# Idle TensorE products in the gaps of a fused SSD and squared-ReLU FFN kernel, with one load and one product group moved

## The chip, the cores and the metric

The kernel runs on one core of one Trainium2 chip. Its time is the device time of one execution in microseconds (us); the median over several executions is what is compared. Each core has TensorE (PE, matrix products, results in PSUM), VectorE (DVE), ScalarE (ACT), GpSimd (POOL) and SyncE (SP). Here SP and POOL issue nearly all DMA transfers. A product is preceded by a weight load, which the profile lists as PEld.

## The reference

A state-space layer (chunked scan with decay) feeds an FFN with a squared ReLU. Cut to what matters:

```python
# x (4,8,768,32)  a (4,8,768)  B, C (4,8,768,16); in chunks of 32 positions
M       = einsum('bhin,bhjn->bhij', Cc, Bc) * exp(cum_i - cum_j) * causal
y_intra = einsum('bhij,bhjd->bhid', M, xc)
y_inter = einsum('bhin,bhnd->bhid', Cc, state) * exp(cum_i)
y       = y_intra + y_inter
state   = exp(sum(log a)) * state + sum_j Bc_j * xc_j * exp(cum_last - cum_j)
# y as (3072, 256), w_in (256, 2048), w_out (2048, 256)
h   = maximum(y @ w_in, 0)
out = (h * h) @ w_out
```

The output is 3072 x 256 in float32.

## The kernel before

The 3072 tokens are cut into 12 pairs, each 256 tokens of one batch (`PAIRS`; two halves of 128 tokens, `u`, with their own state). For each pair k there is a state-space part and an FFN block.

State-space part of pair k, in this order:

- `ph_load`: three DMAs into `C_nat`, `B_nat` and `x_nat` (128, 128 and 256 KB), from a ring of four buffers each (`nat`). SP issues them, only B of pair 0 is issued by ACT.
- `ph_prep` (`prep_c`, `prep_b`, `prep_x`): C times the running decay into `cz`, B cast into `Bb`, x over the running decay into `xs`. For pairs from 2 on POOL does all three; for pairs 0 and 1 ACT does B and DVE does C.
- `ph_tr`: six transposes on PE, copied by DVE into `bct`. `ph_mt`: 16 products of C and B (`mt`). `ph_mask`: four causal masks on DVE into `mts`. For pair 0 two of them read a copy made by ACT (`mtc`).
- `ph_u`: 16 products of B and x (`U`). `ph_s`: DVE makes the states `S` from U and the total decay `Ptot`.
- `ph_y`: first the products of `bct` with the state (line 264), then 32 products of `mts` with `xs` (line 276), all summed in PSUM as `Y`, then evicted into `T`. For pair 0 only the second half has a state.

FFN block of pair b, eight steps f: `mm1` (four 256-wide products `hps` with two of the 16 slices of `w_in`, then a ReLU on ACT into `hb`), `square` (DVE, one step later, into `h`), `mm2` (four products `ops` with two slices of `w_out`, four steps later, `LAG`). At the last step ACT evicts `ops` and SP stores it.

The order is written out by hand (`manual_schedule`), with one running count of steps s = 8b + f. The dictionary `todo` says at which step what part of a later pair is issued; `at(s, ...)` adds to it. Every engine works through its instructions in order and waits for the semaphores that each of them needs; a tile's buffer is taken from a ring (the pool), and the writer waits for the readers of whatever held the buffer before.

Ahead of step 0 there is a stretch by hand: the loads of pairs 0 to 3 on SP; on POOL the constants `cb`, the first quarter of `w_in`, `prep_x(0)`, then the other weights by quarters (`load_wi` in slices 4 to 8, 8 to 12, 12 to 16, `load_wo` in slices 0 to 4, 4 to 8, 8 to 16) with `prep_x(1)` between them. The weights are float32 in memory and bfloat16 in the tiles. `w_in` slices 4 to 8 are first read at step 2, slices 8 to 12 at step 4, 12 to 16 at step 6; `w_out` slices 0 to 4 at step 4, 4 to 8 at step 6, 8 to 16 at step 8.

`warm(n, cols)` issues n products of a tile of zeros, `dum`, into a PSUM tile `dps` that nothing reads: 16 of 256 columns at the start, 3 behind the transposes of the decay (`ptr`), 5 of 128 columns behind `ph_tr(0)` and 14 behind `ph_u(0)`.

Of the kernel before, what the change touches and what calls it, by code (L numbers as in the profile page):

```python
# [10 lines left out]
FP32 = mybir.dt.float32  # L11
# [19 lines left out]
def kernel(  # L31
# [14 lines left out]
    nc = tc.nc  # L46
    NH, S, D, N = 8, 768, 32, 16
    NPAIR = 12
    LAG = 4
    LEAD = 10  # L50

    const = ctx.enter_context(tc.tile_pool(name="const", bufs=1))
    wpool = ctx.enter_context(tc.tile_pool(name="w", bufs=1))
    nat = ctx.enter_context(tc.tile_pool(name="nat", bufs=4))
    prep = ctx.enter_context(tc.tile_pool(name="prep", bufs=3))
    big = ctx.enter_context(tc.tile_pool(name="big", bufs=2))
    tpool = ctx.enter_context(tc.tile_pool(name="tpool", bufs=4))
# [31 lines left out]
    a_nat = const.tile([96, 256], FP32, name="a_nat")  # L89
    a_cl = const.tile([96, 256], FP32, name="a_cl")  # L90
    dum = const.tile([128, 256], BF16, name="dum")
    zer = const.tile([96, 128], FP32, name="zer")
    cp_r = const.tile([96, 256], FP32, name="cp_r")
    pick_p = const.tile([96, 2, 12], FP32, name="pick_p")
# [13 lines left out]
    loaded = {}  # L108
# [17 lines left out]
    def load_wo(f0, f1):  # L126
        nc.gpsimd.dma_start(  # L127
            out=w_out_b[:, f0:f1, :],
            in_=moe_w_out[f0 * 128:f1 * 128, :].rearrange("(f p) d -> p f d", p=128))


    live = {}
# [95 lines left out]
    def ph_s(k, us=(0, 1)):  # L228
# [3 lines left out]
        for u in us:  # L232
# [10 lines left out]
            S_u.append(S_n)  # L243
            state[b] = S_n

    T = {}

    def ph_y(k):
        b, j = PAIRS[k]
        v = live[k]  # L250
        if k < 1:
            Y = [ps_s.tile([128, 2, 128], FP32, tag="A", name=f"Y{k}_{u}", padded_shape=[128, 8, 128])
                 for u in range(2)]
        else:
            t = ps_s.tile([128, 2, 4, 128], FP32, tag="A", name=f"Y{k}")
            Y = [t[:, u, 0:2, :] for u in range(2)]
        first = {(u, q): True for u in range(2) for q in range(4)}
        for u in range(2):
            S_b = v["S"][u]
            if S_b is None:  # L260
                continue
            for g in range(2):
                for q in range(4):
                    nc.tensor.matmul(  # L264
                        Y[u][32 * q:32 * q + 32, g, :],
                        S_b[32 * q:32 * q + 32, g * 32:(g + 1) * 32],
                        _fap(v["bct"][32 * q:32 * q + 32], 128 + g * 128 + u * 64, [[384, 2], [1, 64]]),
                        start=first[(u, q)], stop=False, skip_group_check=True,
                        tile_position=(32 * q, 32 * q))
                    first[(u, q)] = False  # L270
        for g in range(2):
            for r in range(2):
                for u in range(2):
                    for q in range(4):
                        h = 4 * g + q
                        nc.tensor.matmul(  # L276
                            Y[u][32 * q:32 * q + 32, g, :],
                            v["xs"][64 * u:64 * u + 64, r, h * 32:h * 32 + 32],
                            v["mts"][64 * u:64 * u + 64, q, r, g, :],
                            start=first[(u, q)], stop=(g == 1 and r == 1), skip_group_check=True,  # L280
                            tile_position=(64 * u, 32 * q))
                        first[(u, q)] = False
        if 2 <= k < NPAIR - 1:
            ph_u(k + 1)

        T[k] = tpool.tile([128, 2, 2, 2, 64], BF16, tag="T", name=f"T{k}")
        if k < 1:
            for u in range(2):
                o, i = _fap(T[k], u * 64, [[128, 4], [1, 64]]), _fap(Y[u], 0, [[64, 4], [1, 64]])
                if u:  # L290
                    nc.vector.tensor_copy(out=o, in_=i)
                else:
                    nc.scalar.copy(out=o, in_=i)
        else:
            nc.scalar.copy(out=_fap(T[k], 0, [[64, 2], [128, 4], [1, 64]]),  # L295
                           in_=_fap(Y[0], 0, [[512, 2], [64, 4], [1, 64]]))
# [57 lines left out]
    with tc.manual_schedule():  # L354
        nc.sync.dma_start(out=a_nat, in_=_dap(a, 0, [[256, 96], [1, 256]]))
        nc.scalar.dma_start(out=cf, in_=cf_d.ap())
        ph_load(0, "C")
        ph_load(0, "B", nc.scalar)
        ph_load(0, "x")
        nc.gpsimd.dma_start(out=cb, in_=cb_d.ap())  # L360
        load_wi(0, 4)
        for k in (1, 2, 3):
            ph_load(k)

        nc.vector.memset(dum, 0.0)  # L365
        nc.vector.memset(zer, 0.0)
        for i in range(3):
            nc.vector.memset(cz[i], 0.0)
        dps = ps_o.tile([128, 256], FP32, tag="ops", name="dps", padded_shape=[128, 512])

        def warm(n, cols=256):
            for _ in range(n):
                nc.tensor.matmul(dps[:, 0:cols], dum[:, 0:128], dum[:, 0:cols],  # L373
                                 start=True, stop=True, skip_group_check=True)

        warm(16)
        nc.vector.tensor_scalar(out=a_cl, in0=a_nat, scalar1=1e-6, scalar2=1.0, op0=ALU.max, op1=ALU.min)
        for u in range(2):
            nc.vector.tensor_tensor_scan(out=cp_r[:, u * 128:(u + 1) * 128], data0=a_cl[:, u * 128:(u + 1) * 128],
                                         data1=zer, initial=1.0, op0=ALU.mult, op1=ALU.add)  # L380
        nc.vector.tensor_tensor(out=pick_p, in0=_fap(pick, 0, [[0, 2], [1, 12]]),
                                in1=_fap(cp_r, 127, [[128, 2], [0, 12]]), op=ALU.mult)
        ptr = ps_h.tile([128, 2, 96], FP32, tag="hps", name="ptr", padded_shape=[128, 2, 256])
        for r in range(2):
            nc.tensor.transpose(ptr[:, r, :], _fap(cp_r, r, [[2, 128]]), eye_f)
        warm(3)
        pps = ps_h.tile([128, 2, 12], FP32, tag="hps", name="pps", padded_shape=[128, 2, 256])
        nc.tensor.matmul(pps, spread, pick_p, start=True, stop=True)
        nc.scalar.copy(out=P_sb, in_=ptr)
        prep_b(0, nc.scalar)  # L390
        nc.scalar.copy(out=Ptot, in_=pps)
        prep_c(0, nc.vector)
        nc.vector.reciprocal(out=_fap(Pinv, 0, [[96, 2], [3, 32]]), in_=_fap(P_sb, 0, [[96, 2], [3, 32]]))
        prep_x(0, nc.gpsimd)
        load_wi(4, 8)
        load_wo(0, 4)
        load_wi(8, 12)
        load_wo(4, 8)
        ph_tr(0)
        warm(5, 128)  # L400
        ph_mt(0)
        mtc = big.tile([128, 2, 2, 2, 128], BF16, tag="mtc", name="mtc", bufs=1)
        for i in (1, 0):
            nc.scalar.copy(out=mtc[:, i], in_=live[0]["mt"][1][:, i])
        ph_mask(0, 0)
        ph_u(0)
        warm(14, 128)
        ph_mask(0, 1)
        ph_s(0, (0,))
        ph_mask(0, 3, mtc[:, 1])  # L410
        ph_mask(0, 2, mtc[:, 0])
        prep_b(1, nc.scalar)
        prep_c(1, nc.vector)
        prep_x(1, nc.gpsimd)
        load_wi(12, 16)
        load_wo(8, 16)
        ph_y(0)
        ph_s(0, (1,))

        steps = [(b, f) for b in range(NPAIR) for f in range(8)]  # L420
        todo = {}

        def at(s, fn, *args):
            todo.setdefault(max(s, 0), []).append((fn, args))

        def recip_rest():
            nc.vector.reciprocal(out=_fap(Pinv, 1, [[96, 2], [3, 32], [1, 2]]),
                                 in_=_fap(P_sb, 1, [[96, 2], [3, 32], [1, 2]]))

        at(5, recip_rest)  # L430
        for k in range(1, NPAIR):
            s0 = {1: 0, 2: 7}.get(k, 8 * k - LEAD)
            if k >= 4:
                at(s0 - 15, ph_load, k)
            if k >= 2:
                at(s0 - {2: 6, 3: 5}.get(k, 7), ph_prep, k)
            at(s0, ph_tr, k)
            if k <= 2:
                at(s0 + 1, ph_u, k)
            at(s0 + 1 if k <= 2 else s0 - 1, ph_s, k)  # L440
            at(s0 + 2, ph_mt, k)
            for q in range(4):
                at(s0 + 2 + (q + 1) // 2, ph_mask, k, q)
            at(s0 + (5 if k == 1 else 6), ph_y, k)
        for s in range(len(steps) + LAG):
            if s < len(steps):
                mm1(*steps[s])
            for fn, args in todo.pop(s, []):
                fn(*args)
            if 1 <= s < len(steps) + 1:  # L450
                square(*steps[s - 1])
            if LAG <= s < len(steps):
                mm2(*steps[s - LAG])
        mm2_last(NPAIR - 1, [f for _, f in steps[len(steps) - LAG:]])
# [30 lines left out]
```

## Time and profile before

| what | value |
|---|---|
| median of 6 runs | 128.56 us (127.26 to 129.69) |
| profiled execution: its time | 128.67 us |
| profiled execution: its span | 126.9 us, 4221 instructions |
| mean granted TensorE clock | 0.946 |
| PE busy | 116.1 us (91%) |
| DVE, ACT, POOL busy | 88.4, 72.4, 32.1 us |
| chain that ended last | PE 70%, DMA 12%, DVE 11%, POOL 2% |

The span runs from the first instruction to the last; the rest of the execution's time lies around it. Busy time of PE is modelled and its instructions overlap, so a full PE in a slice says that it has no gap there. The granted clock is the share of full speed that the throttle gave TensorE. The chain is followed back from the last instruction, at each step to what released it. In the timeline's rows the first number is the start, the second the length, and brackets hold the idle time of the engine ahead of the row and what ended it.

### The profile page before, as it was taken

To read this page: it belongs to the slowest core of one execution; us is meant where nothing else is said; L and a number is where in the kernel's file an instruction comes from. 1 tells how busy PE (TensorE), PEld (TensorE's weight loads), DVE (VectorE), ACT (ScalarE), POOL (GpSimd) and SP (SyncE) were. 2 spreads that over 40 slices of the span, in tenths; PEclk is the share of its full clock that TensorE was granted. 3 is DMA by queue.
4 is the path that set the end of the run, shared out by engine and by line. 5 is a ranking of instruction groups with operands and counts; after the bars stand their busy time and mean duration, and the time that the engine had idled before them with its cause. 6 is when DMAs were issued, how large, how long until landed. Compare 5 with 4: busy or idle time off the path is not lost.

```text
span 126.9 us, 4221 instructions
## 1 busy us (share of the span) xinstructions
PE 116.1 (91%) x1778; PEld 92.7 (73%) x1778; DVE 88.4 (70%) x207; ACT 72.4 (57%) x129; POOL 32.1 (25%) x54
## 2 busy tenths in 40 slices
PE   6747849999999999999999999999999999999970
PEld 4525415778778978787888789788888887788840
DVE  3666588179989679599798795794865957934520
ACT  4232332456558557657576485585585675867720
POOL 5049942164052060430430430511500000000000
PEclk9997555699999999999999999999999999999999
DMA  4999999970830743905606507317220020020211
GB/s 81 205 196 148 185 206 214 212 141 3 182 71 10 161 85 92 161 5 132 121 3 152 101 0 167 86 52 138 64 83 8 0 90 3 5 83 0 88 41 41
DMA packets 42788, 12.10 MB, mean 95 GB/s; under 512 B 37808, under 2 KB 41344, under 8 KB 42768
## 3 DMA queue, kind: packets, MB, share of 16 engines
q1 hardware_dynamic: 38240, 9.28, 36.4%
q0 software_dynamic: 3232, 2.20, 12.0%
q10 hardware_dynamic: 1296, 0.35, 1.3%
q8 instruction: 14, 0.23, 0.7%
q14 instruction: 6, 0.05, 0.1%
HBM read 10.77 MB, written 3.15 MB: 110 GB/s over the span
## 4 chain that ended last, share of the span: by engine, by line
PE 70%; DMA 12%; DVE 11%; POOL 2%; ACT 1%; SPq 1%; issue 1%; DVEq 0%; POOLq 0%
PE ops L326 29%; PE hps L306 28%; DMA w_in_b<-in_moe_w_in_dram 7%; DVE mts L201 6%; DMA x_nat<-in_x_dram 5%; DVE h L316 5%; PE Y L276 3%; PE mt L190 3%; PE Y L264 2%; PE tr L178 2%; PE ops L339 1%; PE U L219 1%; PE tr L176 1%; POOL xs L157 1%; POOL w_out_b L127 1%
## 5 line engine op out<-in xcount | busy, mean ns | idle before, releaser
L310 ACT ACTIVATE hb<-hps 128x512 bf16<-128x512 f32 x96 | 57.5, 599 | 40.1 <-PE hps L306 39.1
L306 PE MATMUL hps<-T,w_in_b 128*128 128x256 bf16 x384 | 60.7, 283 | 2.8 <-DMA w_in_b<-in_moe_w_in_dram 1.7
L326 PE MATMUL ops<-w_out_b,h 128*128 128x256 bf16 x368 | 56.4, 277 | 0.0
L316 DVE TENSOR_TENSOR h<-hb 128x512 bf16<-128x512 bf16 x96 | 43.1, 472 | 6.5 <-ACT hb L310 6.5
L306 PEld LDWEIGHTS <-w_in_b 128*128 128x128 bf16 x384 | 38.3, 101 | 9.2 <-DMA w_in_b<-in_moe_w_in_dram 2.8
L326 PEld LDWEIGHTS <-h 128*128 128x128 bf16 x368 | 34.2, 99 | 6.6 <-issue 2.2
L201 DVE TENSOR_TENSOR mts<-mt,cb 128x512 bf16<-128x512 f32 x46 | 30.4, 682 | 8.3 <-PE mt L190 8.3
L137 POOL TENSOR_TENSOR cz<-C_nat,P_sb 128x256 bf16<-128x256 f32 x10 | 7.0, 696 | 42.9 <-DMA C_nat<-in_C_dram 36.7
L157 POOL TENSOR_TENSOR xs<-x_nat,Pinv 128x512 bf16<-128x512 f32 x12 | 13.0, 1083 | 10.3 <-DMA x_nat<-in_x_dram 10.1
L180 DVE COPY bct<-tr 128x768 bf16<-128x768 bf16 x12 | 6.7, 558 | 12.0 <-PE tr L178 11.7
L151 POOL CAST Bb<-B_nat 128x128 bf16<-128x128 f32 x20 | 6.4, 347 | 5.2 <-DMA B_nat<-in_B_dram 5.2
L295 ACT CAST T<-Y 128x512 bf16<-128x512 f32 x11 | 6.4, 586 | 1.7 <-PE Y L276 1.4
L351 ACT COPY osb<-ops 128x512 f32<-128x512 f32 x11 | 6.4, 579 | 0.0
L276 PE MATMUL Y<-mts,xs 64*32 64x128 bf16 x384 | 6.0, 226 | 0.4 <-DVE mts L201 0.3
L373 PE MATMUL dps<-dum 128*128 128x256 bf16 (+1 forms) x38 | 5.3, 301 | 1.1 <-DVE dum L365 1.1
L190 PE MATMUL mt<-bct 32*64 32x256 bf16 x192 | 5.3, 291 | 0.4 <-DVE bct L180 0.4
L178 PE MATMUL tr<-cb,cz 128*128 128x128 bf16 x48 | 5.6, 227 | 0.0
L176 PE MATMUL tr<-cb,Bb 128*128 128x128 bf16 x24 | 4.9, 228 | 0.4 <-ACT Bb L149 0.4
L373 PEld LDWEIGHTS <-dum 128*128 128x128 bf16 x38 | 3.7, 119 | 2.0 <-DVE dum L365 1.1
L276 PEld LDWEIGHTS <-xs 64*32 64x32 bf16 x384 | 3.4, 93 | 2.2 <-issue 1.0
L219 PE MATMUL U<-xs,Bb 64*32 64x64 bf16 x160 | 3.5, 199 | 1.5 <-POOL xs L157 1.5
L242 DVE TENSOR_SCALAR S<-z,Ptot 128x64 bf16<-128x64 f32 x16 | 4.3, 270 | 0.6
(40 smaller groups left out, 45.0 us busy)
## 6 DMA issues: line engine op xcount, KB each, us to landing
x_nat<-in_x_dram SPq DMA_DIRECT2D x12, 256.0 KB, 4.4
out_dram<-osb SPq DMA_DIRECT2D x11, 256.0 KB, 2.3
C_nat<-in_C_dram SPq DMA_DIRECT2D x12, 128.0 KB, 3.8
B_nat<-in_B_dram SPq DMA_DIRECT2D x11, 128.0 KB, 4.3
w_in_b<-in_moe_w_in_dram POOLq DMA_DIRECT2D x4, 256.0 KB, 7.2
w_out_b<-in_moe_w_out_dram POOLq DMA_DIRECT2D x2, 256.0 KB, 8.6
w_out_b<-in_moe_w_out_dram POOLq DMA_DIRECT2D x1, 512.0 KB, 11.9
B_nat<-in_B_dram ACTq DMA_DIRECT2D x1, 128.0 KB, 4.5
```

The source lines that it names most:

```text
L137: eng.tensor_tensor(out=_fap(czk, 0, [[240, 2], [32, 8], [1, 16]]), in0=_fap(loaded[k]["C"], 0, [[16, 2], [32, 8], [1, 16]]), in1=_fap(P_s ...
L157: eng.tensor_tensor(out=_fap(xs, 0, [[256, 2], [32, 8], [1, 32]]), in0=_fap(loaded[k]["x"], 0, [[32, 2], [64, 8], [1, 32]]), in1=_fap(Pinv ...
L178: nc.tensor.transpose(tr[:, r, 1 + g, :], v["cz"][:, r, 112 * g:112 * g + 128], eye_b)
L180: nc.vector.tensor_copy(out=bct, in_=tr)
L190: nc.tensor.matmul(mt[q // 2][64 * u:64 * u + 64, q % 2, r, :, :], bct[32 * q:32 * q + 32, r, 0, u * 64:u * 64 + 64], _fap(bct[32 * q:32 * ...
L201: nc.vector.tensor_tensor(out=v["mts"][:, q], in0=v["mt"][q // 2][:, q % 2] if src is None else src, in1=_fap(cb, 128, [[128, 2], [0, 2], ...
L276: nc.tensor.matmul(Y[u][32 * q:32 * q + 32, g, :], v["xs"][64 * u:64 * u + 64, r, h * 32:h * 32 + 32], v["mts"][64 * u:64 * u + 64, q, r, ...
L306: nc.tensor.matmul(hps[:, i, :], w_in_b[:, g, f * 128:(f + 1) * 128], T[blk][:, g].rearrange("p r u t -> p (r u t)"), start=(g == 0), stop ...
L310: nc.scalar.activation(out=hb, in_=hps, func=AF.Relu)
L316: nc.vector.tensor_tensor(out=h2, in0=hb, in1=hb, op=ALU.mult)
L326: nc.tensor.matmul(ops[blk][:, r, :], h2[:, i, r * 128:(r + 1) * 128], w_out_b[:, f, :], start=(f == 0 and r == 0), stop=(f == 15), skip_g ...
L373: nc.tensor.matmul(dps[:, 0:cols], dum[:, 0:128], dum[:, 0:cols], start=True, stop=True, skip_group_check=True)
```

## The change

- `warm` is called in more places: behind `pps` 4 products of 128 columns (and 1 in place of 3 of 256 columns ahead of it), behind `ph_tr(0)` 12 in place of 5, behind `ph_mt(0)` 22, behind `ph_y(0)` 9, and 4 behind `mm1` in steps 1, 2 and 3.
- The `nat` ring has three buffers in place of four. The load of pair 3 stands behind the last weight load, with three one-column copies on POOL from pair 0's `C_nat`, `B_nat` and `x_nat` into a scratch tile `touch` ahead of it.
- For pair 0 the `mts` products go ahead of the products with the state. DVE does the masks of pair 0 from `mtc` ahead of the state of its first half.
- Pair 3: transposes at step 15 (14 before), U in a place of its own at step 16 (before: inside Y of pair 2, step 13), state at step 16 (13), and so `mt`, masks and Y one step later; its prep at step 11 (9). The load of pair 4 stands at step 10 (7).

```diff
-    nat = ctx.enter_context(tc.tile_pool(name="nat", bufs=4))
+    nat = ctx.enter_context(tc.tile_pool(name="nat", bufs=3))
...
+    def y_intra(k, Y, first, last):
+        v = live[k]
+        for g in range(2):
+            for r in range(2):
+                for u in range(2):
+                    for q in range(4):
+                        h = 4 * g + q
+                        nc.tensor.matmul(
+                            Y[u][32 * q:32 * q + 32, g, :],
+                            v["xs"][64 * u:64 * u + 64, r, h * 32:h * 32 + 32],
+                            v["mts"][64 * u:64 * u + 64, q, r, g, :],
+                            start=first[(u, q)], stop=(last and g == 1 and r == 1), skip_group_check=True,
+                            tile_position=(64 * u, 32 * q))
+                        first[(u, q)] = False
...
+        if k == 0:
+            y_intra(k, Y, first, False)
         for u in range(2):
...
-        for g in range(2):
-            for r in range(2):
...
-        if 2 <= k < NPAIR - 1:
+        if k > 0:
+            y_intra(k, Y, first, True)
+        if 3 <= k < NPAIR - 1:
             ph_u(k + 1)
...
-        for k in (1, 2, 3):
-            ph_load(k)
+        ph_load(1)
+        ph_load(2)
...
-        warm(3)
+        warm(1)
...
+        warm(4, 128)
         ph_tr(0)
-        warm(5, 128)
+        warm(12, 128)
         ph_mt(0)
+        warm(22, 128)
...
         ph_u(0)
         warm(14, 128)
         ph_mask(0, 1)
-        ph_s(0, (0,))
         ph_mask(0, 3, mtc[:, 1])
         ph_mask(0, 2, mtc[:, 0])
+        ph_s(0, (0,))
...
         load_wi(12, 16)
         load_wo(8, 16)
+        for what in "CBx":
+            nc.gpsimd.tensor_copy(out=touch, in_=loaded[0][what][:, 0, 0:1])
+        ph_load(3)
         ph_y(0)
+        warm(9, 128)
         ph_s(0, (1,))
...
-            s0 = {1: 0, 2: 7}.get(k, 8 * k - LEAD)
+            s0 = {1: 0, 2: 7, 3: 15}.get(k, 8 * k - LEAD)
             if k >= 4:
-                at(s0 - 15, ph_load, k)
+                at(s0 - (12 if k == 4 else 15), ph_load, k)
             if k >= 2:
-                at(s0 - {2: 6, 3: 5}.get(k, 7), ph_prep, k)
+                at(s0 - {2: 6, 3: 4}.get(k, 7), ph_prep, k)
             at(s0, ph_tr, k)
-            if k <= 2:
+            if k <= 3:
                 at(s0 + 1, ph_u, k)
-            at(s0 + 1 if k <= 2 else s0 - 1, ph_s, k)
+            at(s0 + 1 if k <= 3 else s0 - 1, ph_s, k)
...
                 mm1(*steps[s])
+            if 1 <= s < LAG:
+                warm(4, 128)
```

More of the change, by code (lines that the diff above doesn't have):

```diff
@@ L91 @@
     dum = const.tile([128, 256], BF16, name="dum")
+    touch = const.tile([128, 1], FP32, name="touch")
     zer = const.tile([96, 128], FP32, name="zer")
@@ L267, in ph_y @@
                         _fap(v["bct"][32 * q:32 * q + 32], 128 + g * 128 + u * 64, [[384, 2], [1, 64]]),
-                        start=first[(u, q)], stop=False, skip_group_check=True,
+                        start=first[(u, q)], stop=(k == 0 and g == 1), skip_group_check=True,
                         tile_position=(32 * q, 32 * q))
                     first[(u, q)] = False
-        for g in range(2):
-            for r in range(2):
[L273 to L282, printed above, removed]
-        if 2 <= k < NPAIR - 1:
+        if k > 0:
+            y_intra(k, Y, first, True)
+        if 3 <= k < NPAIR - 1:
             ph_u(k + 1)
```

## The prediction

> **What bounds the kernel now.** I read the page's 40 slices first, then the chain of waits in order of time, then the PE timeline up to 27 us, then the clock in fine windows.
>
> ```profile
> PE   6747849999999999999999999999999999999970
> PEclk9997555699999999999999999999999999999999
> ```
>
> Each digit is 3.17 us. From slice 9 on PE is full and its clock is full. All that a change of the start can win lies before 32 us, and there the granted clock is 0.5 in slices 5 to 7. The chain of waits says what sets the order in that stretch:
>
> ```profile
> 1.65 6.27 DMA x_nat<-in_x_dram
> 8.06 1.06 POOL xs L157
> 9.12 0.72 POOL w_in_b L122
> 9.84 0.75 POOL w_out_b L127
> 10.59 8.50 DMA w_in_b<-in_moe_w_in_dram
> 19.13 1.04 PE hps L306 x4
> 20.17 0.85 PE ops L326 x4
> ```
>
> Up to 19.13 us no PE instruction is on the chain: the pair-0 load of x, its scaling on POOL, the issue of the weights behind it, and the landing of the third quarter of w_in (issued 10.59, landed 19.09) decide when FFN step 4 starts. The PE rows show the same from PE's side:
>
> ```profile
> 9.17 0.25 PE L219 MATMUL U<-xs,Bb 64*32 64x64 bf16 x16 [1.51 <-POOL xs L157]
> 14.86 1.03 PE L306 MATMUL hps<-T,w_in_b 128*128 128x256 bf16 x4 [0.45 <-ACT hb L310]
> 19.13 1.04 PE L306 MATMUL hps<-T,w_in_b 128*128 128x256 bf16 x4 [1.69 <-DMA w_in_b<-in_moe_w_in_dram]
> 24.91 0.60 PE L306 MATMUL hps<-T,w_in_b 128*128 128x256 bf16 x4
> 32.51 0.41 PE L276 MATMUL Y<-mts,xs 64*32 64x128 bf16 x29 [0.29 <-DVE mts L201]
> ```
>
> The same four products take 1.04 us at 19.13 and 0.60 at 24.91: that is the clock. In 0.2 us windows it is
>
> ```profile
> 10.90:11.10 0.20, 0.09 (x13) 0.00 (x0) 0.00 (x0) 0.06 (x1) 0.20 (x1) 0.56 1.47 133
> 24.40:24.60 0.20, 0.20 (x3) 0.14 (x2) 0.00 (x0) 0.00 (x0) 0.20 (x2) 0.55 1.31 248
> ```
>
> (the third number from the end is the clock). 0.56 puts the fall at 10.92, 0.55 the return at 24.58. So from 19.13 to 24.58, 5.45 us, PE sets the pace at half clock. This is the only stretch where idle products can pay.
>
> **The sum.** The profiled execution took 128.67 us, its span 126.9; 1.77 lie around it. The median shown is 128.56, 0.11 below it, and I take gains off the median.
>
> *The clock, if it stays full.* I walk PE from 19.13 with the full-clock rows: 0.44 for four 256-wide products (33.43 to 33.87), 0.34 for the six transposes (33.87 to 34.21), 0.45 for Y (half of 21.80 to 22.69), 0.19 for U (26.65 to 26.84). hps step 4 ends 19.57, ops 20.01, hps step 5 20.45, Y 20.90, ops 21.34. Step 6 needs the last quarter of w_in: issued 13.07, 8.9 us to landing, so 22.0. Then hps 22.46, ops 22.90, hps 23.34, tr 23.68, ops 24.12, hps 24.56, U 24.75. The next ops needs the last half of w_out, issued 13.83, 11.9 us to landing: 25.73, start 25.75. In the trace this ops (step 4 of block 0) starts at 26.84. Gain 1.09; the weights take back the rest. Behind it PE runs without a gap up to the 0.29 wait for DVE's masks in Y of pair 2. DVE gets its tr and mt earlier too, so that wait can go: 0 to 0.29. Upper bound of the gain 1.38, lower bound 0 (clock as before).
>
> *Does the clock stay?* The 22 products before ph_u(0) fill the 1.51 wait: the 14 of the same form took 0.96, 69 ns each, so 22 take 1.5 and end at 9.2 where U starts at 9.17. The 4 and the 12 fill 0.38 and 0.37 waits, the 9 (0.62) the 0.69 wait at step 0. So the fall at 10.92 should go. But full clock opens new waits, because the weights set steps 2 and 4. From 11.67: hps 0.44, tr 0.34, hps 0.44, four idle products 0.28, then U, which needs xs of pair 1 (POOL until 13.14): PE is done near 13.4 and step 2 waits for w_in (issued 9.08, 5.7 to landing) until 14.85. That is 1.45 idle, and the idle products of a step stand behind its hps, so they wait with it. Step 2 and 3 then take 0.44 + 0.28 + 0.42 (mt) + 0.44 + 0.28 and end near 16.7; step 4 waits until 19.13: 2.4 idle. Before, a wait of 1.51 was followed by a lost clock, waits of 0.38 and 0.37 were not. By these rows the 2.4 wait costs the clock, and after 19.13 it would come back as before. The return needed a long unbroken run. Cut into stretches of 3.41 us (a quarter of the time from fall to return; the first number behind the length is PE's busy time), the 3.42 before the fall had 1.91 busy; 2.72 and 2.65 did not bring the clock back, 3.41 did:
>
> ```profile
> 7.51:10.93 3.42, 1.91 (x86) 1.45 (x70) 2.57 (x6) 1.57 (x4) 2.87 (x4) 1.00 1.26 192
> 10.93:14.34 3.41, 2.72 (x38) 1.80 (x30) 1.49 (x4) 1.10 (x3) 3.40 (x5) 0.50 1.08 139
> 14.34:17.75 3.41, 2.65 (x38) 1.06 (x24) 2.56 (x6) 1.34 (x3) 2.78 (x5) 0.50 1.40 206
> 21.17:24.58 3.41, 3.41 (x53) 1.99 (x52) 1.01 (x3) 1.18 (x2) 0.61 (x3) 0.50 1.56 211
> ```
>
> [...] I take a share of executions in which the clock is full for part or all of 19.13 to 24.58, and price that at half of the 1.09: 0.55.
>
> [...]
>
> *The fourth pair's loads.* Three DMAs (128, 128 and 256 KB) are meant to start behind the weights. SP's order is unchanged: they stay its tenth to twelfth issues, only waits are added. With three buffers instead of four they overwrite an earlier pair, and in the built program's waits they do not wait for the touches on POOL: the ring gives them pair 1's buffers (the touches made pair 0's the later ones to come free), so C waits for DVE's cz of pair 1, B for ACT's Bb of pair 1, x for POOL's xs of pair 1. Those end at 10.86, 10.1 and 13.14; before, SP issues:
>
> ```profile
> 10.40 0.69 SPq L116 DMA_DIRECT2D C_nat<-in_C_dram  x1
> 11.13 3.88 SPq L116 DMA_DIRECT2D B_nat<-in_B_dram  x1
> 15.06 2.50 SPq L116 DMA_DIRECT2D x_nat<-in_x_dram  x1
> ```
>
> DVE now does cz of pair 1 after masks and S in a new order with the same total, so C moves by 0 to 0.46 us, B and x by nothing: SP was held 3.88 us in B's issue anyway. Pair 4 waits for the touches (near 15.1), before its first issue at 17.68. So the traffic is as before and w_in lands at 19.09 as before. Price 0; if the loads did leave the stretch, what they moved before 19.09 is at most C (128 KB, landed 20.7); at the 205 GB/s of the slices that is 0.6 us, the upper bound of a gain.
>
> *POOL's touches.* Three 128x1 copies, between 0.10 (a 128x1 memset) and 0.35 each (a 128x128 cast), 0.3 to 1.05, ahead of pair 2's prep. Behind them: cz, Bb, xs of pair 2. POOL idles 0.44 before that xs and its reader U starts at 26.65, xs ended at 17.57. Price 0; without that cover 1.05.
>
> *Pair 0's products in another order.* The 32 mts products need masks (done near 9.7), the 8 S products S; both stand behind the 14 idle products that end at 10.3. Same end near 10.95. Price 0, covered by the 19.13 landing.
>
> *Pair 3 one to three steps later* (tr 15, U and S 16, mt 17, Y 21; T is read at step 24). No work is added. Its mt now waits for S reading U one step before, as pair 2's does now: U 26.65, z done 27.57, mt 27.82, 0.25 of slack. If DVE stands one square later (0.41), PE loses 0.16. On the other side S of pair 3 (0.83) leaves DVE's fullest stretch. Bounds -0.29 to +0.3, value 0. The load of pair 4 at step 10 instead of 7 is not seen by SP, whose order is the same.
>
> Sum: 128.56 - 0.55 = 128.0.
>
> **Rivals.**
> 1. *The clock holds throughout* (0.22). For it: no unfilled wait as early as before. Against it: the 2.4 wait. 1.38 off: 127.2.
> 2. *Nothing moves* (0.20): the clock is lost in the wait for step 4 in nearly every execution, and the loads do not leave the stretch. 128.5.
> 3. *Slower* (0.10): the idle products meet a half clock and become a queue. The first 16 took 3.39 for 256 columns each, 0.212, so 0.106 for 128. With 12 + 22 + 14 + 9 + 12 of them cold: mt ends 8.6, 22 more 10.9, U 11.2, 14 more 12.7, Y 13.6, 9 more 14.5, hps + tr + hps 2.33 to 16.9, four more and U 17.6, hps, four more, mt 19.5, hps and four more 20.8. Step 4 is 1.65 late: 130.2. It decides once cold products hold more than about 60% of that stretch (2.6 of slack at full clock against 4.3 of added time). [...]
>
> **How the numbers follow.** Forecast 128.0 with 0.48, its own range 127.5 to 128.4. Range for 8 in 10: low 126.9 (rival 1 with 0.3 of the unknown price of the loads), high 129.2 (rival 2 with the +0.3 of pair 3 and the spread of before). About 1%, 1.29 us, is what a measurement of this kernel can tell from no change. Faster than 127.27 comes from most of rival 1, 0.20; slower than 129.85 from most of rival 3, 0.07; the rest 0.73.
>
> **What would show it.** Right: no 1.51 gap before U, clock 1.00 at 11 to 17, PE waits for w_in still ending near 14.85 and 19.1, pair 3's loads issued at 10 to 15 us. Whether the clock is 1.00 or 0.50 in 19 to 24.6 tells forecast and rival 1 from rival 2; ops of step 4 should then start at 25.8 behind w_out. Wrong: step 4 starting clearly before 18.5 (the loads did matter) or after 19.5 (the idle products delay work).

## The result, and the profile after

The changed kernel takes 127.54 us in the median of 37 executions (126.56 to 129.53), the kernel before 128.01 in the median of 79 (126.56 to 129.92). The ratio is 0.9979, interval 0.9962 to 0.9995: a gain of about 0.27 us, where 0.55 was forecast. A second set of 12 executions gave 0.9976 (0.9944 to 1.0009). Ratios here leave out executions more than 1.5% above the fastest of their kernel. The profiled execution took 127.04 us, its span 125.3, against 128.67 and 126.9 before.

The page's 40 slices after, with PE's busy tenths and the granted clock:

```profile
PE   6999448699999999999999999999999999999970
PEclk9999999999999999999999999999999999999999
```

The three slices at 0.5 are gone. PE's gaps are not: they stand in slices 5 to 8 (12.5 to 25 us, counted from 1) now. The chain of waits after, the pieces of the start that matter:

```profile
7.93 1.06 POOL xs L158
...
13.70 12.15 DMA w_out_b<-in_moe_w_out_dram
25.85 0.04 issue
25.89 0.60 PE ops L334 x4
```

Before, the chain passed from the weights to PE at 19.13, for FFN step 4. Now it stays with the weights until 25.85, the landing of the last half of w_out for step 8. The PE timeline after shows each wait on the way:

```profile
9.22 0.25 PE L220 MATMUL U<-xs,Bb 64*32 64x64 bf16 x16
15.01 0.61 PE L314 MATMUL hps<-T,w_in_b 128*128 128x256 bf16 x4 [1.68 <-DMA w_in_b<-in_moe_w_in_dram]
18.75 0.61 PE L314 MATMUL hps<-T,w_in_b 128*128 128x256 bf16 x4 [1.78 <-DMA w_in_b<-in_moe_w_in_dram]
22.86 0.61 PE L314 MATMUL hps<-T,w_in_b 128*128 128x256 bf16 x4 [1.52 <-DMA w_in_b<-in_moe_w_in_dram]
25.89 0.60 PE L334 MATMUL ops<-w_out_b,h 128*128 128x256 bf16 x4 [0.15 <-DMA w_out_b<-in_moe_w_out_dram]
31.03 0.42 PE L254 MATMUL Y<-mts,xs 64*32 64x128 bf16 x32
```

The 1.51 us wait before U has no bracket any more, since idle products fill it. Four products take 0.61 at 18.75 where they took 1.04. But steps 2, 4 and 6 each wait 1.5 to 1.8 us for w_in. The last row had a 0.29 wait for DVE before and has none now.

### The profile page after: what moved, and what is told of

Read it like the earlier page. It is cut to its first block, busy times and chain, and to the rows that moved or that the text cites. A ratio compares the mean times of both kernels' runs of the same rounds, so it can differ in the third digit from the quotient of the medians.

```text
span 125.3 us, 4329 instructions
## 1 busy us (share of the span) xinstructions
PE 114.8 (92%) x1830; PEld 93.6 (75%) x1830; DVE 86.5 (69%) x207; ACT 72.4 (58%) x129; POOL 32.0 (26%) x57
## 4 chain that ended last, share of the span: by engine, by line
PE 75%; DMA 15%; POOL 4%; ACT 1%; issue 1%; DVE 1%; SPq 1%; DVEq 0%; POOLq 0%
PE ops L334 32%; PE hps L314 30%; DMA w_out_b<-in_moe_w_out_dram 10%; DMA x_nat<-in_x_dram 5%; PE Y L254 3%; PE mt L191 3%; PE Y L282 2%; POOL xs L158 2%; PE tr L179 2%; POOL w_in_b L123 1%; POOL w_out_b L128 1%; PE ops L347 1%; PE U L220 1%; PE tr L177 1%; ACT hb L318 0%
## 5 line engine op out<-in xcount | busy, mean ns | idle before, releaser
L314 PE MATMUL hps<-T,w_in_b 128*128 128x256 bf16 x384 | 57.6, 273 | 5.0 <-DMA w_in_b<-in_moe_w_in_dram 5.0
L334 PE MATMUL ops<-w_out_b,h 128*128 128x256 bf16 x368 | 55.4, 273 | 0.2 <-DMA w_out_b<-in_moe_w_out_dram 0.2
L324 DVE TENSOR_TENSOR h<-hb 128x512 bf16<-128x512 bf16 x96 | 41.1, 453 | 5.8 <-ACT hb L318 5.8
L314 PEld LDWEIGHTS <-w_in_b 128*128 128x128 bf16 x384 | 37.1, 98 | 10.1 <-DMA w_in_b<-in_moe_w_in_dram 5.5
L381 PE MATMUL dps<-dum 128*128 128x128 bf16 (+1 forms) x90 | 9.6, 261 | 1.1 <-DVE dum L373 1.1
L381 PEld LDWEIGHTS <-dum 128*128 128x128 bf16 x90 | 7.1, 110 | 2.3 <-DVE dum L373 1.1
L152 POOL CAST Bb<-B_nat 128x128 bf16<-128x128 f32 x20 | 5.5, 302 | 5.7 <-DMA B_nat<-in_B_dram 3.0
L254 PE MATMUL Y<-mts,xs 64*32 64x128 bf16 x384 | 5.2, 219 | 0.0
L242 DVE TENSOR_TENSOR z<-U,S 128x64 f32<-128x64 f32 x16 | 3.6, 223 | 2.0 <-PE U L220 1.7
L282 PE MATMUL Y<-bct,S 32*32 32x128 bf16 x160 | 4.4, 217 | 0.0
```

Source lines behind the costliest of these rows:

```text
L254: nc.tensor.matmul(Y[u][32 * q:32 * q + 32, g, :], v["xs"][64 * u:64 * u + 64, r, h * 32:h * 32 + 32], v["mts"][64 * u:64 * u + 64, q, r, ...
L282: nc.tensor.matmul(Y[u][32 * q:32 * q + 32, g, :], S_b[32 * q:32 * q + 32, g * 32:(g + 1) * 32], _fap(v["bct"][32 * q:32 * q + 32], 128 + ...
L314: nc.tensor.matmul(hps[:, i, :], w_in_b[:, g, f * 128:(f + 1) * 128], T[blk][:, g].rearrange("p r u t -> p (r u t)"), start=(g == 0), stop ...
L324: nc.vector.tensor_tensor(out=h2, in0=hb, in1=hb, op=ALU.mult)
L334: nc.tensor.matmul(ops[blk][:, r, :], h2[:, i, r * 128:(r + 1) * 128], w_out_b[:, f, :], start=(f == 0 and r == 0), stop=(f == 15), skip_g ...
```

## The experiments

Each was timed beside the kernel before on the same chip, and the ratio is to that. Kernels of different sets are compared by these ratios. Every execution also gave its mean granted clock: 1.000 is a clock not lost after it came up (at 6.43 us in the profile after), and a stretch of 3.41 us at half clock, a quarter of the 13.66 from fall to return in the profile of before, takes some 0.0136 off (half of 3.41 in 125.3). By that sum 0.985 leaves no more than 3.8 us at half clock. In 87 executions of before the median clock is 0.959, and 15 have 0.985 or more. In 50 of the changed kernel 35 have 0.985 or more and none less than 0.967.

**Fill alone (two runs).** The kernel before with every `warm` call of the change:

```diff
-        warm(3)
+        warm(1)
...
-        warm(5, 128)
+        warm(12, 128)
         ph_mt(0)
+        warm(22, 128)
```

(and 4 ahead of `ph_tr(0)`, 9 behind `ph_y(0)`, 4 in steps 1 to 3).

> The kernel before with all the idle products of the change and nothing else of it (four load buffers, old order for pair 0 and pair 3). Theory A, the fill keeps the clock and is all of the effect: a median near the changed kernel's 127.5 us, ratio to before 0.995 to 1.000, mean granted clock 0.967 or more in nearly every execution (as in 37 executions of the changed kernel). Rival B, the moved loads and the new order bring it: 128.0 us, ratio 1.00, and mean clocks down to 0.946 as in the profile of before.

> The kernel e1_fill_only again (all idle products, nothing else), to halve the uncertainty of its share. If the fill is the whole effect of the change: 0.2 to 0.5 us below before. If the effect needs the other parts too: within 0.15 us of before. Mean clocks 0.967 or more in either case.

Measured: 127.60 us, ratio 1.0006 (0.9968 to 1.0044), then 127.78 us, 0.9988 (0.9949 to 1.0027). Two executions, of 284 and 164 us, are left out of ratios and clocks; what made them long is not known. The clock is up: 17 of the other 22 at 0.985 or more, none below 0.967. So the fill by itself does what it is meant to do to the clock, and the time hardly follows: no gain that these intervals can tell from none. The gain of 0.2 to 0.5 us expected of the fill as the whole effect did not show.

**No fill (two runs).** The changed kernel with 3, 5 and 14 idle products as before (the 9 and those of steps 1 to 3 are out too):

```diff
-        warm(4, 128)
         ph_tr(0)
-        warm(12, 128)
+        warm(5, 128)
         ph_mt(0)
-        warm(22, 128)
```

> The changed kernel with the idle products of before (3, 5 and 14) in place of its own; loads, order and pair 3 stay changed. Theory A: 128.0 us, ratio 1.00, mean clock often below 0.96. Rival B: 127.5 us. Rival C, the order costs something that the fill pays for: 128.3 or more.

> The kernel e2_no_fill again (the other parts of the change, idle products as before). Its first run was 0.67 us above before in the mean (128.45 against 127.78), with an error of 0.26. If the other parts cost something alone: 0.4 to 0.9 above before again. If that was chance: within 0.3 of before.

Measured: 128.60 us, 1.0011 (0.9963 to 1.0059), then 127.85 us, 1.0029 (0.9993 to 1.0065); 16 of 24 clocks are below 0.967, as with before. The other parts alone bring nothing; whether they cost something is not settled. Between this kernel and the changed one, 1.0011 and 1.0029 against 0.9979 and 0.9976, the fill is worth 0.3 to 0.5%. That it is worth so much only beside the other parts, and not alone, the intervals do not prove, and I leave it open.

The second profile without fill shows how little a lost clock can cost. Four 256-wide products take 0.60 us at 12.35 in it, 0.79 at 15.17, 1.03 to 1.06 from 16.47 to 20.82, and 0.61 at 22.54 (mean clock 0.969); in its PE timeline step 8 starts at

```profile
25.97 0.60 PE L334 MATMUL ops<-w_out_b,h 128*128 128x256 bf16 x4
```

which is 0.08 us behind the 25.89 of the profile that never lost it. The landing of w_out, at 25.85 in that profile, covers the rest up to there. The whole span is 0.4 us longer than in that profile (125.7 against 125.3).

**The 22 products only.**

```diff
         ph_mt(0)
+        warm(22, 128)
```

> The kernel before with one edit: 22 idle products of 128 columns behind the mt products of pair 0, which fill the 1.51 us wait for POOL's xs. Theory A1, this wait alone loses the clock: mean clocks as in the changed kernel (0.967 or more) and 127.5 to 127.7 us. Rival A2, the clock is lost by the sum of several waits: clocks between the two, 127.8 us.

Measured: 128.55 us, ratio 1.0028 (0.998 to 1.0075), clocks 0.96 to 0.985 in 10 of 12 executions. A1 fails by its time, and its clocks lie between before and the changed kernel, as A2 said; the time is above both theories. The PE timeline of this run shows where the clock goes when only the first wait is filled:

```profile
15.67 0.59 PE L190 MATMUL mt<-bct 32*64 32x256 bf16 x16
16.19 1.03 PE L306 MATMUL hps<-T,w_in_b 128*128 128x256 bf16 x4
```

The products slow down inside mt (0.59 us, against 0.42 for pair 0's at 7.26), after the waits that follow U, instead of at 10.92. That this is the work of the 22 is not shown: the profile without fill above, which lacks them, also lost its clock only in the products at 15.17. The clocks show that the other idle products are needed: 2 of 12 executions at 0.985 or more here, 17 of 22 with all of them.

**Pair 3 held behind the issue of the weights.** Four buffers, and instead of the touches a write by POOL into the tile that the load then waits for:

```diff
+            if held:
+                nc.gpsimd.memset(dst[:, 0, 0:1], 0.0)
             (eng or nc.sync).dma_start(
```

> The changed kernel with pair 3's load held until POOL has issued the last weights (near 14.6 us), by a one-column write of POOL into each of pair 3's three tiles; four load buffers, no touches. This is what the change says it does with that load, but waits for the issue of the weights and not for their landing. Theory R, the queue of pair loads works in order and reaches pair 3 only when pair 2 has landed (near 16.2 us), so an issue at 14.6 moves nothing: the changed kernel's 127.2 to 127.8 us, ratio to before 0.995 to 1.000. Rival: the later issue frees the weights, as in e6_land3: 126.3 to 126.9 us.

Measured: 127.14 us, ratio 0.9958 (0.9926 to 0.999). The ratio fits theory R, and the median is not in the 126.3 to 126.9 of the rival. The interval leaves room for a small gain over the changed kernel.

**Pair 3 held behind the landing of the weights.** Again four buffers and no touches. The write into each tile now copies from the last slice of w_out, so it waits for that slice, and stands at step 2:

```diff
+            if behind is not None:
+                nc.gpsimd.tensor_copy(out=dst[:, 0, 0:1], in_=behind)
...
+        at(2, ph_load, 3, "CBx", None, w_out_b[:, 15, 0:1])
```

> The changed kernel with the load of pair 3 really behind the weights: four load buffers, no touches, and a one-column copy on POOL from the last slice of w_out into each of pair 3's tiles, behind pair 2's prep, so that the loads wait until the last weights have landed. Theory W, with the clock up the landings of the weights set steps 4 to 8, and pair 3's traffic delays them: w_in for step 4 lands 0.3 to 0.6 us before the 18.7 of the changed kernel, w_in for step 6 at 20.8 to 21.5 instead of 22.8, the last w_out at 23.5 to 24.3 instead of 25.85; median 125.8 to 126.6 us. Rival V, the transfers only change places and pair 4 or pair 3 comes late: 127.3 us or more.

Measured: 126.85 us, ratio 0.9896 (0.986 to 0.9933). The SP timeline shows that the load left the stretch:

```profile
25.02 0.37 SPq L119 DMA_DIRECT2D C_nat<-in_C_dram  x1
```

In that profile the last w_out landed 11.1 us after an issue at 13.69, so at 24.8 instead of 25.85, and PE does not wait at step 6 or 8. But in the profiled execution four products take 0.71 us at 15.58, 1.03 to 1.06 from 17.23 to 21.14 and 0.61 at 22.93: it had lost its clock in between, which made PE late there by itself, and took 127.61. Theory W holds in sign of the time. For step 4 the landing did not come forward (PE starts it at 19.46, where 18.3 was expected and the changed kernel had 18.75), and the median is 0.25 above the forecast's end. In SP's rows pair 4's load stands behind it and moved back as well: its C from 19.00 in the changed kernel to 26.92. The gain is that of both loads. The same kernel without fill:

> The kernel e6_land3 with the idle products of before (3, 5, 14). If the weights' landings hide the lost clock, earlier landings uncover it: the fill should be worth more here than in the changed kernel, 0.7 to 1.5 us, so 126.8 to 127.8 us with mean clocks below 0.96. Rival: the fill is worth no more than 0.3 us here either, because a clock lost before step 4 comes back by itself.

Measured: 127.18 us, ratio 0.9945 (0.9914 to 0.9976), clock median 0.958. The fill is worth 0.5% here, 0.6 us, a little under the 0.7 to 1.5 expected and over the rival's 0.3. The two intervals overlap, so whether it is worth more here than in the changed kernel is not settled.

**The last half of w_out in two DMAs.**

```diff
-        load_wo(8, 16)
+        load_wo(8, 12)
+        load_wo(12, 16)
```

> The kernel e6_land3 with the last half of w_out loaded in two DMAs of four slices, since step 8 needs the first of them alone. If the last w_out is the landing that holds step 8 (PE waits there in e6_land3): 0.3 to 0.9 us less than e6_land3. If not: the same, or 0.2 more for one more issue on POOL.

Measured: 126.34 us in 7 executions, ratio 0.9902 (0.986 to 0.9943), against 0.9896: the same. Step 8 was no longer the wait, step 6 in this profile still was, shortly:

```profile
21.81 0.61 PE L316 MATMUL hps<-T,w_in_b 128*128 128x256 bf16 x4 [0.42 <-DMA w_in_b<-in_moe_w_in_dram]
24.62 0.61 PE L336 MATMUL ops<-w_out_b,h 128*128 128x256 bf16 x4
```

This profile did not lose its clock ahead of step 8 (1.00 from 11 to 31 us), so it shows better than the last where the held load pays: steps 2 and 4 start at 15.39 and 18.80, no earlier than in the changed kernel, step 6 1.05 us and step 8 (the second row) 1.27 us earlier.

**Pair 2 held as well.** The changed kernel with the loads of pairs 2 and 3 both held behind the weights' issue (the `memset` above):

```diff
+        ph_load(2, held=True)
+        ph_load(3, held=True)
```

> The changed kernel with four load buffers in which the loads of pairs 2 and 3 are held on SP until POOL has issued the last weights (a one-column write by POOL into each of the six tiles, which the load then waits for; the three touches are gone). Theory W, at full clock the weights' landings set steps 2, 4 and 6: the profile of the changed kernel has 1.68, 1.78 and 1.52 us of PE waits for w_in there; without the 512 KB of pair 2 in the queue before 16.2 us w_in for step 2 should land 1 to 2 us earlier than 15.0 and for step 4 1 to 2.5 us earlier than 18.75, and the whole should take 125 to 126.7 us. Rival V, the transfers only change places: pair 2 then lands after 20 us, its transposes wait, and the time is 127.5 to 129 us.

Measured: 130.55 us, ratio 1.0207 (1.0157 to 1.0258). That is above the ranges of both theories. Its PE timeline has both in it:

```profile
13.99 0.61 PE L316 MATMUL hps<-T,w_in_b 128*128 128x256 bf16 x4 [0.36 <-DMA w_in_b<-in_moe_w_in_dram]
17.57 0.61 PE L316 MATMUL hps<-T,w_in_b 128*128 128x256 bf16 x4 [1.63 <-DMA w_in_b<-in_moe_w_in_dram]
21.19 0.61 PE L316 MATMUL hps<-T,w_in_b 128*128 128x256 bf16 x4 [1.03 <-DMA w_in_b<-in_moe_w_in_dram]
25.45 0.29 PE L179 MATMUL tr<-cb,Bb 128*128 128x128 bf16 x1 [2.77 <-POOL Bb L154]
```

Steps 2, 4 and 6 start 1.0, 1.2 and 1.7 us earlier than in the changed kernel, and then pair 2's transposes wait 2.77 us for its B. What the weights gain, pair 2 gives back with interest; behind that wait this execution also ran at half clock: four products take 0.60 us at 22.08, 1.06 at 26.06 and still 1.03 at 30.55.

**One weight load issued earlier.** The split kernel with one line moved:

```diff
+        load_wi(4, 8)
         prep_x(0, nc.gpsimd)
-        load_wi(4, 8)
```

> The kernel e7_land3_split with one line moved: the second quarter of w_in is issued by POOL ahead of prep_x(0), so near 2.7 us instead of 9. In e7_land3_split PE still waits 1.91 us for it at step 2 and 1.46 for the third quarter at step 4. Theory W: it lands near 12 to 13.5 instead of 15.4, each later quarter 0.5 to 2 us earlier, pair 2's x later by as much; median 124.8 to 125.9 us. Rival V: the load of x of pair 0 or 1 is delayed by the new traffic and the first steps start later: 126.3 us or more.

Measured: 125.77 us, ratio 0.9838 (0.9796 to 0.988), the fastest of all: 1.6% below before. The interval overlaps a little with that of the split kernel. In its PE timeline

```profile
13.54 0.61 PE L316 MATMUL hps<-T,w_in_b 128*128 128x256 bf16 x4
18.11 0.61 PE L316 MATMUL hps<-T,w_in_b 128*128 128x256 bf16 x4 [2.61 <-DMA w_in_b<-in_moe_w_in_dram]
21.97 0.61 PE L316 MATMUL hps<-T,w_in_b 128*128 128x256 bf16 x4 [1.27 <-DMA w_in_b<-in_moe_w_in_dram]
```

step 2 no longer waits, and steps 4 and 6 still do. Against the split kernel's profile step 4 starts 0.69 us earlier, but step 6 0.16 later (21.97 against 21.81), and the two profiled executions took the same (125.75 and 125.80 us). So what the moved line is worth beside the split kernel is not settled. The clock is at 0.985 or more in five of six executions.

**The changed kernel again**, beside the set of the landing experiments:

> The changed kernel again, on the same chip and beside the same executions of before as the others of this set. Theory A (the fill keeps the clock, which pays only in the executions of before that lose four windows of 3.41 us, and little in the others): median 127.2 to 127.8, mean clock 0.967 or more, 0.2 to 0.5 us below before.

Measured: 127.63 us, ratio 0.9976 (0.9944 to 1.0009), as expected. Its step 8 started at 26.50 behind w_out, 0.61 us later than in the other profile of the same kernel: the landings, too, differ between executions. This profile caught an execution that lost the clock; PE's busy time is the first number behind the length, the clock the third from the end:

```profile
12.23:15.64 3.41, 1.58 (x33) 1.30 (x31) 1.69 (x5) 1.13 (x2) 3.29 (x7) 1.00 1.13 172
15.64:19.05 3.41, 2.63 (x31) 1.51 (x29) 2.12 (x4) 1.19 (x2) 1.86 (x4) 0.50 1.54 208
19.05:22.47 3.42, 3.42 (x52) 2.12 (x52) 2.53 (x7) 1.19 (x2) 0.63 (x1) 0.50 1.63 213
```

## Why the prediction was right, and where it was off

*The walk at full clock* was right in its mechanism: step 8 was to start at 25.75 behind w_out and starts at 25.89 behind it; the 0.29 wait of Y is gone. The waits for w_in moved as forecast to steps 2 (14.85, measured 15.01), 4 (19.13, measured 18.75) and 6, but there the landing came 0.86 us later than forecast (22.0, measured 22.86). Of the 1.0 us that PE was to wait at step 8 this left 0.15, so that the late landing did not show in the sum. That the walk came out to 0.14 us is in part luck: the second profile of the same kernel has 26.50. In the two profiles the span fell by 1.6 us, a little over the upper bound of 1.38; they are a pair of which one had half clock for 13.66 us and the other kept it from 6.43 on.

*The size.* The sum forecast 0.55, half of the 1.09, and 0.27 was measured. The half was the author's estimate and no run shows it; the runs show a clock of 0.985 or more in 35 of 50 executions of the changed kernel, and in 15 of 87 of before. Which term was off is not settled. The 1.09 came from one execution of before in which the clock was at half for 13.66 us and returned as late as 24.58. That is the costly case, not the usual one: 27 of 87 executions of before have a clock below 0.953, as it has, and in the profile that had full clock again at 22.54 step 8 is 0.08 us late. Of the 69 executions of before in the ratios, those with a clock of 0.985 or more average 127.29 (13 executions, standard error 0.17), all of them 127.65. A clock that is hardly ever lost is then worth some 0.36 us on average, and the changed kernel's 127.46 is about there. Those groups can differ in more than the clock, so this is an observation; it fits a kernel that was mostly limited by the landings of the weights. By it the 0.55 was too large. The direct test, fill against no fill beside the other parts, gives 0.3 to 0.5%, or 0.4 to 0.6 us. By that the 0.55 was about right, and it was the parts priced at 0 that cost 0.1 to 0.4 us (1.0011 and 1.0029, neither told from 1 by its interval). The fill alone, at 1.0006 and 0.9988, speaks for the first reading. The level was off as well: six executions gave 128.56 for before, 79 gave 128.01. So the median of 127.54 lies in the forecast's own range by the level more than by the gain.

*Does the clock stay?* This step argued from the rows that a 2.4 us wait must cost the clock, since one of 1.51 had. The wait for step 4 measured 1.78, and in that profile it cost nothing. The windows of the profile after, counted in stretches of 3.41 us from 6.43, where the trace's clock record has the clock come up (four idle products take 0.60 us at 5.85 and 0.39 at 12.76):

```profile
13.26:16.67 3.41, 1.73 (x46) 1.27 (x31) 1.54 (x5) 0.89 (x2) 3.29 (x9) 1.00 1.28 201
16.67:20.09 3.42, 1.64 (x17) 1.21 (x15) 3.42 (x8) 1.19 (x2) 0.72 (x1) 1.00 1.57 212
20.09:23.50 3.41, 1.89 (x52) 1.25 (x51) 1.52 (x4) 1.18 (x2) 0.64 (x1) 1.00 1.69 213
```

Three stretches in a row with less PE work than the 1.91 that preceded the fall before, and the clock stays at 1.00. The forecast's cover for this, that some executions keep the clock and some lose it, is what happened: 35 of 50 have 0.985 or more, the other 15 are from 0.968 to 0.984. In the execution of the fence before this section the clock fell at 15.64, after a stretch with 1.58 us of PE work.

*The moved loads.* The forecast said that the touches would not hold pair 3's load back. The SP timeline after:

```profile
10.52 0.84 SPq L117 DMA_DIRECT2D C_nat<-in_C_dram  x1
11.47 3.38 SPq L117 DMA_DIRECT2D B_nat<-in_B_dram  x1
14.95 4.00 SPq L117 DMA_DIRECT2D x_nat<-in_x_dram  x1
```

They stand close to the 10.40, 11.13 and 15.06 of before. Holding the load at the issue of the weights (the fourth experiment) moved its first issue only to 14.91, and little in the time. The bound put on a load that really leaves, 0.6 us, was too small: from the changed kernel's 0.9979 to 0.9896 it brought 0.8%, about 1.0 us, pair 4's later load included. The bound counted only what the load moved before the third quarter of w_in landed, and left out the fourth quarter and w_out. The split kernel's profile shows these as the ones that came forward, by 1.05 us at step 6 and 1.27 at step 8.

*The rest.* The touches took 0.19 to 0.20 us each, within the bounds, and pair 2's xs ended at 17.39, covered as said. In the profile after U did not start late (9.22 against 9.17) and Y of pair 0 ended as before; their price of 0 was not tested alone, nor was that of pair 3's later steps. Of the rivals, the clock held throughout in the profiled execution, but the average gain was far from 1.38. The second, a clock lost in nearly every execution, did not come: 26 of 50 have 0.99 or more. The queue of cold products did not appear: the 22 behind mt take 1.40 us at 7.89, where the third rival had 2.3.

## What to carry to other kernels

A lost clock cost little where PE did not set the pace: 0.08 us at step 8 in the second profile without fill. So walk the engine at full speed against the landings of what it needs, and take the smaller of the two gains. With the clock up, the waits that it hid were the next price here, 1.68, 1.78 and 1.52 us for w_in; moving a 512 KB load, and the one behind it, past the landing of the weights brought three to four times what the idle products and the rest of the change brought together. Holding a load at the issue of the weights moved little for pair 3, issued at 10 to 15 us anyway, but 1.0 to 1.7 us of the starts that wait for weights with pair 2 held as well, whose own readers then waited 2.77. The waits of the built program tell which buffer, and so whose readers, a load really waits for.

## What was not expected of the hardware

In three profiles, of before, of the changed kernel and the second of the changed kernel, the amount of PE work does not say by itself when the clock is lost. In the profile after, stretches with 1.73, 1.64 and 1.89 us of PE's modelled work in 3.41 or 3.42 kept it at 1.00. In that of before it fell at 10.92 behind a stretch with 1.91 of 3.42, and in the second profile of the changed kernel at 15.64 behind one with 1.58 of 3.41. At half clock, stretches with 2.72, 2.65 and 2.04 us did not bring it back in before, nor did one with 2.63 in the second profile of the changed kernel; the full clock followed one with 3.41 of 3.41 in the former (at 24.58) and one with 3.42 of 3.42 in the latter (four products take 0.61 us at 22.57). The place in the kernel differs too. The clock record has full clock from 4.10 us in before and from 6.43 in the profile after, and of two executions of the changed kernel one lost the clock at 15.64 and the other not at all behind 6.43. What else decides, the kind of the products or something that the model of PE's time misses, these runs do not tell.
